# The first tile's decay factors: picked as logarithms for two chunks at once, masked by a product, and the opening of the kernel put into another order

## The chip, the cores and the metric

The kernel runs on one core of a Trainium2 chip. The metric is the device time of one execution in microseconds (us); several executions are timed and their median is taken. Engines are called as in the profile: PE (TensorE, with PEld for its weight loads), DVE (VectorE), ACT (ScalarE), POOL (GpSimd), SP (SyncE, which here only issues DMAs).

## What is computed

A state-space attention over 4 batches and 8 heads, in chunks of the 768 positions, then two feed-forward blocks on the 3072 tokens.

```python
cum = np.cumsum(la, axis=-1)                       # la = log(clip(a))
L = np.exp(cum[:, :, :, None] - cum[:, :, None, :]) * causal
M = np.einsum('bhin,bhjn->bhij', Cc, Bc) * L
y_intra = np.einsum('bhij,bhjd->bhid', M, xc)
y_inter = np.einsum('bhin,bhnd->bhid', Cc, state) * np.exp(cum)[..., None]
state = decay_full * state + sum_j(B_j x_j decay_from_j)
# x: y as [3072, 256]
h = relu(x @ w_in) ** 2;  x = h @ w_out                # d_ff 2048
h = (x @ w1) * (x @ w2) @ w3;  out = h @ w_out2        # d_ff 1024
```

## The kernel before, in words

Tokens go in 6 tiles of 512, the attention in chunks of 96 positions. Tile 0 needs chunks 0 to 5, which make up units 0, 1, 2 of two chunks each. `startup()` computes them in an order that is written out by hand (everything in it is chained engine by engine by `in_order`). After it `step()` runs phase A of tile 0: for each of 16 slices m of the hidden width `h_mm` (PE, L808, 6 products of 512 columns), relu and square (ACT, L822 and L830), a split of the square into a high part (ACT, L838) and a low part (DVE, L139), and `x2_mm` (PE, L855, 6 products) some slices later. Matrices are handled as a high and a low fp32r part, three products for one.

**Weights.** They come as 64-bit words in pieces of 512 KB (`conv_load`, tile names `ua`, then `uo`, `u`). A piece is made into two fp32r parts: `conv_words` (ACT, two instructions, L195 and L197, into `cvs` or `cv`), `conv_bits` (DVE, L206 and L209), `conv_parts` (high part by ACT or POOL, L229 and L227, low part by DVE, L139, into `wa`). Startup converts pieces 0 to 2 and takes the words of piece 3; step m converts piece 3 + m and takes the words of piece 4 + m. Piece j is needed by slice j.

**Tile 0 in startup.** `decays_e_first` (L380) makes the logarithms of the decay rows with 27 small fp32 products out of `lp` (the logs) and `m_rel`/`m_oth` (0/1 masks), and ACT's exp writes them to `e_first`; `decays_cols` (L431) makes the other factors, `dec`. For each unit `unit_g0` (L620) makes C times B in four PSUM banks, `unit_gm` copies them to SBUF with the causal mask (two by DVE, L631, two by ACT, L635, and POOL masks these), `chunk_pick` (L646) spreads four heads' rows of `e_first` over the partitions by a product with a 0/1 matrix `pick`, and `chunk_m0` (DVE, L671) multiplies the picked rows with the masked C times B. `chunk_pre` (POOL, L554) scales x and B of a chunk; `chunk_ds` (L703) makes the chunk's state, `chunk_hand` (ACT, L712, four copies) writes it under the next chunk's x, `chunk_y_mm` (L743) makes y and `chunk_out` splits it into `xt`, the input of phase A.

**Tile 1's chunks** 6 to 10 go another way beside phase A: `unit_split` splits B and C of a unit into high and low (`hl`, ACT L142 and DVE L139), SP stores `hl` to DRAM (`hl_d`), and `unit_bc` reads it back in 12 small DMAs (`bt` x6, `cb` x6).

**What sets the order of the loads.** All DMAs are issued by SP, in the program's order (`dma()` keeps it), and a DMA whose source is not ready holds all behind it. They use eight semaphores in turn, so that a DMA is issued only when the one eight places ahead has landed. In the program's order the store of unit 3's `hl` comes right before weight piece 3, then two small loads of `raw`, then the 12 reads of that store, chunk 6's x, weight piece 4, the store of unit 4, and so on.

Of the kernel before, what the change touches and what calls it, by code (L numbers as in the profile page):

```python
# [46 lines left out]
GPB = 4  # L47
TMPB = 6
# [8 lines left out]
def kernel(  # L57
# [93 lines left out]
    cmask = act1.tile([P, P], F32, tag="cmask", name="cmask")[:, :CH]  # L151
# [130 lines left out]
    lp = new_tmp()[:, :192].rearrange("p (k c) -> p k c", k=3)  # L282

    def constants():
        def diagonal(v):
            nc.gpsimd.affine_select(
                out=v, in_=v, pattern=[[0, v.shape[1]], [-1, v.shape[2]]], base=0, channel_multiplier=1,
                compare_op=ALU.not_equal, fill=1.0,
            )

        nc.gpsimd.memset(ident, 0.0)
        diagonal(ident.unsqueeze(1))
        for k, eng in enumerate((nc.vector, nc.gpsimd)):
            eng.tensor_copy(
                pick[k].rearrange("r h (p j) -> r h p j", p=4),
                ident.rearrange("r (p k h) -> r k h p", p=4, k=4)[:, k].unsqueeze(3).to_broadcast([P, H, 4, 32]),
            )
        nc.gpsimd.memset(cmask, 1.0)
        causal(cmask.unsqueeze(1))
# [6 lines left out]
        nc.gpsimd.memset(cb.bitcast(F32), 0.0)  # L306

    def decays_load(k):
# [4 lines left out]
        else:  # L313
            dma(out=m_oth[:, :392], in_=masks[:, 512:904])

    def decays_ln():
# [3 lines left out]
        )  # L320
        warm = const.tile([P, 1], F32, name="warm")
# [50 lines left out]
    e_first = wts.tile([P, 4, CH], F32, tag="w127", name="e_first")  # L372

    def decays_e_first():

        pv = new_mm()[:, :4 * CH].rearrange("r (v i) -> r v i", v=4)

        def put_e(v, p, i, n, *terms):
            for x, (kk, rhs) in enumerate(terms):
                nc.tensor.matmul(  # L380
                    pv[32 * p:32 * p + 32, v, i:i + n], lp[:, kk, :32], rhs, start=(x == 0),
                    stop=(x == len(terms) - 1), skip_group_check=True,
                )
# [148 lines left out]
    def causal(m):  # L532
# [4 lines left out]
            fill=0.0,  # L537
# [49 lines left out]
    def unit_bi(c0, c1):  # L587
        nc.scalar.copy(bi[:, c0:c1, :CH], batch_0[0][:, c0 * CH:c1 * CH].rearrange("p (c i) -> p c i", i=CH))
# [18 lines left out]
    gm = {}  # L607
    GM_PLACE = ("wo0", "wo1", "wo2", "wo3", "wa10", "wa11")
# [16 lines left out]
    def unit_gm(u, i):  # L625

        gm[u, i] = t = wts.tile([P, 2, 4, CH], F32, tag=GM_PLACE[2 * u + i], name="gm")
        for k in range(2):
            ps = g0[u][2 * i + k][:, :4 * CH].rearrange("p (c i) -> p c i", c=4)
            if i == 0:  # L630
                nc.vector.tensor_tensor(  # L631
                    out=t[:, k], in0=ps, in1=cmask.unsqueeze(1).to_broadcast([P, 4, CH]), op=ALU.mult
                )
            else:
                nc.scalar.copy(t[:, k], ps)  # L635
        if i == 1:
            causal(t.rearrange("p q c i -> p (q c) i"))

    picked = {}

    def chunk_pick(g, i):

        k, v = divmod(g, 4)
        picked[g, i] = ps = new_mm()[:, :4 * CH].rearrange("p (h i) -> p h i", h=4)
        for h in range(4):
            nc.tensor.matmul(  # L646
                ps[:, h], pick[k][:, 4 * i + h], e_first[:, v], start=True, stop=True, skip_group_check=True,
            )

    def unit_e0(u):  # L650
        if u < 2:
            t = at.tile([P, 2, H * CH], F32, tag="e", name="e")
            tiles = [t[:, 0], t[:, 1]]
        else:
            tiles = [wts.tile([P, H * CH], F32, tag=f"w12{2 + k}", name="e") for k in range(2)]
        for g, t in zip(UNITS[u], tiles):
            es[g] = t.rearrange("p (h i) -> p h i", h=H)

    def chunk_e(g, i):

        u, j = UNIT[g]
        if g not in es:
            e = at.tile([P, 2, H * CH], F32, tag="e", name="e")
            for k, gg in enumerate(UNITS[u]):
                es[gg] = e[:, k].rearrange("p (h i) -> p h i", h=H)
        chunk_pick(g, i)
        nc.scalar.copy(es[g][:, 4 * i:4 * i + 4], picked.pop((g, i)))

    def chunk_m0(g, i):
        u, j = UNIT[g]  # L670
        nc.vector.tensor_tensor(  # L671
            out=es[g][:, 4 * i:4 * i + 4].rearrange("p (q h) i -> p q h i", q=2),
            in0=picked.pop((g, i)).rearrange("p (q h) i -> p q h i", q=2), in1=gm[u, i][:, :, 2 * j:2 * j + 2, :],
            op=ALU.mult,
        )
# [22 lines left out]
    def chunk_ds(g, s):  # L698
# [3 lines left out]
        for q in range(4):  # L702
            keep(nc.tensor.matmul(  # L703
                s[32 * q:32 * q + 32], pb[:n, q], xb[:n, 64 * q:64 * q + 64],
                start=True, stop=True, skip_group_check=True,
            ))
# [31 lines left out]
    def chunk_y_mm(g, ys):  # L738
        ch = chs[g]
        for hg in range(2):  # L740
            for q in (2, 3, 0, 1):
                h = 2 * q + hg
                keep(nc.tensor.matmul(  # L743
                    ys[32 * q:32 * q + 32, hg], ch["xb"][:, 32 * h:32 * h + 32], es[g][:, h],
# [14 lines left out]
    def chunk_y(g):  # L759

        yp = y_bank[:, g % 2 * 256:g % 2 * 256 + 256]
        ys, s = yp[:, :2 * CH].rearrange("p (h i) -> p h i", h=2), yp[:, 2 * CH:]
# [3 lines left out]
        if g + 1 == FIRST[2]:  # L766
            s2 = y_bank[:, 448:512]
# [237 lines left out]
    def attention_plan_1():  # L1005
# [26 lines left out]
    def startup():  # L1032
        ys = {}

        def y0(g):
            ys[g] = ps_acc.tile([P, 512], F32, tag="acc", name="y")[:, :2 * CH].rearrange("p (h i) -> p h i", h=2)
            chunk_y_mm(g, ys[g])

        s = y_bank
        ds = [s[:, 64 * (g % 4):64 * (g % 4) + 64] for g in range(FIRST[1])]  # L1040
        constants()
# [3 lines left out]
        batch_load(0)  # L1045
        batch_load(1)
        chunk_xb(0)
        conv_load(1)
        chunk_xb(1)
        chunk_xb(2)  # L1050
        for g in range(3, FIRST[1]):
            chunk_xb(g, f"w12{1 + g}")
        unit_load(4)
        conv_load(1)
        for u in range(3):
            unit_e0(u)
        decays_ln()
        nc.vector.tensor_copy(halves, m_oth[:, 384:392].rearrange("p (q h) -> p h q", h=2)[:, :, 0])
        for q in range(1, 4):
            nc.vector.tensor_tensor(  # L1060
                out=halves, in0=halves, in1=m_oth[:, 384 + 2 * q:386 + 2 * q], op=ALU.add
            )
        nc.scalar.copy(bi[:, :, CH:], id2.unsqueeze(1).to_broadcast([P, FIRST[1], 32]))
        decays_e_first()
        unit_bi(0, 2)
        unit_pad(0)
        decays_cols()
        unit_g0(0)
        unit_bi(2, 6)
        unit_pad(1)  # L1070
        conv_load(1)
        unit_load(5)
        chunk_pre(0)
        unit_gm(0, 0)
        unit_gm(0, 1)
        chunk_pre(1)
        unit_pad(2)
        chunk_pick(0, 0)
        chunk_pick(0, 1)
        unit_g0(1)  # L1080
        chunk_ds(0, ds[0])
        chunk_m0(0, 0)
        chunk_pick(1, 0)
        chunk_m0(0, 1)
        chunk_hand(0, ds[0])
        unit_gm(1, 0)
        unit_gm(1, 1)
        chunk_pre(2)
        unit_split(3, "w120")
        unit_rows(bt)  # L1090
        conv_load(1)
        unit_bc(3)
# [211 lines left out]
```

## Time and profile before

| | |
|---|---|
| time, median of 3 | 567.51 us (567.03 to 569.09) |
| span of the profiled execution | 566.8 us |
| first product of phase A | at 30.88 us |
| first cast of tile 0's result `x` (end of its phase A) | at 94.60 us |
| PE busy | 549.4 us, 97% of the span |
| DVE, ACT, POOL busy | 363.3, 291.9, 90.8 us |

The profiled execution lies 0.7 us below the median. Times in the rows count from the span's start. Busy shares are means over stages with different limits, so the first 100 us are read by stretches below. A line "x16" of a fp32 product counts two instructions for each product of the program, a fp32r product is one.

### The profile page before, as it was taken

What the parts mean: (1) busy time and instruction counts of PE and PEld (TensorE: products, weight loads), DVE (VectorE), ACT (ScalarE), POOL (GpSimd) and SP (SyncE); (2) the same over time, 40 slices, a digit from 0 to 9 for tenths busy, and PEclk for the clock granted to TensorE, in tenths of its full rate; (3) what the DMA queues carried; (4) which work ended last, traced back from release to release, by engine and by line L of the source; (5) the groups of instructions that cost most, each with busy time, mean ns of one, the idle gap of its engine ahead of it and who ended that gap; (6) DMA issues with size and microseconds to landing.
All of it is one profiled execution on the core that took longest, in us unless ns stands there. A gap on an engine that the chain in (4) does not pass through costs nothing.

```text
span 566.8 us, 9839 instructions
## 1 busy us (share of the span) xinstructions
PE 549.4 (97%) x3682; PEld 465.0 (82%) x3682; DVE 363.3 (64%) x651; ACT 291.9 (52%) x579; POOL 90.8 (16%) x138
## 2 busy tenths in 40 slices
PE   6999979999999999999999999999999999999997
PEld 5877757789988888888888988888888888888887
DVE  4888999887999564466666465655466474545431
ACT  5899857877976242263433354333444333544332
POOL 5636650000000212004021004020002010000000
PEclk9999999999999999999999999999999999999999
DMA  8697692043354652057251066120072220100001
GB/s 224 194 321 205 209 378 86 8 162 127 126 193 118 147 138 76 1 139 172 64 123 43 1 164 153 43 78 1 21 195 79 57 71 1 38 1 0 1 2 37
DMA packets 48560, 59.51 MB, mean 105 GB/s; under 512 B 22912, under 2 KB 36608, under 8 KB 48512
## 3 DMA queue, kind: packets, MB, share of 16 engines
q1 hardware_dynamic: 48512, 58.88, 35.9%
q8 instruction: 29, 0.48, 0.4%
q14 instruction: 19, 0.16, 0.1%
HBM read 50.20 MB, written 8.65 MB: 104 GB/s over the span
## 4 chain that ended last, share of the span: by engine, by line
PE 77%; DMA 8%; DVE 8%; SPq 3%; ACT 2%; issue 2%; ACTq 0%; DVEq 0%
PE mm L808 39%; PE acc L855 18%; PE acc L908 10%; PE mm L256 4%; SPq L91 3%; DMA raw<-in_raw_dram 2%; PE y L743 2%; DMA u<-in_w_dram 2%; PE g L599 2%; DMA hl_d<-gp 2%; DVE gp L139 1%; DMA e_d<-tmp 1%; PE mm L646 1%; DVE cvs L206 1%; DVE cvs L209 1%
## 5 line engine op out<-in xcount | busy, mean ns | idle before, releaser
L808 PE MATMUL mm<-xt,wa 128*128 128x512 f32 x576 | 147.2, 393 | 4.2 <-DVE wa L139 3.2
L838 ACT CAST gp<-tmp 128x512 fp32r<-128x512 f32 x144 | 89.5, 621 | 115.4 <-DVE tmp L896 62.8
L855 PE MATMUL acc<-gp,wa 128*128 128x512 f32 x576 | 146.4, 392 | 1.7 <-ACT gp L838 1.1
L139 DVE TENSOR_TENSOR gp<-tmp,gp 128x512 fp32r<-128x512 f32 x144 | 102.5, 712 | 63.3 <-ACT gp L838 63.0
L808 PE MATMUL mm<-x,w 128*128 128x512 f32 x576 | 142.6, 393 | 0.0
L808 PEld LDWEIGHTS mm<-xt,wa 128*128 128x128 f32 x576 | 105.2, 188 | 27.4 <-DVE wa L139 5.3
L855 PEld LDWEIGHTS acc<-gp,wa 128*128 128x128 f32 x576 | 106.3, 188 | 24.1 <-ACT gp L838 1.5
L808 PEld LDWEIGHTS mm<-x,w 128*128 128x128 f32 x576 | 104.5, 188 | 20.5 <-ACT tmp L888 0.2
L822 ACT ACTIVATE tmp<-mm 128x512 f32<-128x512 f32 x96 | 57.3, 597 | 54.7 <-PE mm L808 54.4
L908 PEld LDWEIGHTS acc<-w3o,gp 128*128 128x128 f32 x576 | 75.8, 190 | 4.6 <-DVE gp L139 0.3
L908 PE MATMUL acc<-w3o,gp 128*128 128x256 f32 x576 | 78.5, 283 | 0.1
L832 DVE TENSOR_TENSOR tmp<-tmp 128x512 f32<-128x512 f32 x68 | 47.5, 698 | 30.7 <-ACT tmp L822 30.2
L896 DVE TENSOR_TENSOR tmp<-tmp,mm 128x512 f32<-128x512 f32 x48 | 32.9, 685 | 48.6 <-PE mm L808 44.9
L535 POOL TENSOR_SCALAR_AFFINE_SELECT e<-e 96x768 f32<-96x768 f32 x26 | 25.5, 993 | 234.0 <-DMA e<-e_d 187.8
L888 ACT COPY tmp<-mm 128x512 f32<-128x512 f32 x48 | 28.1, 586 | 45.3 <-PE mm L808 44.8
L554 POOL TENSOR_TENSOR xb<-xb,dec 96x256 f32<-96x256 f32 x32 | 23.5, 733 | 101.0 <-DMA xb<-in_xb_dram 44.2
L605 DVE TENSOR_TENSOR e<-g,e 128x384 f32<-128x384 f32 x52 | 27.6, 550 | 6.0 <-PE g L599 4.7
L256 PE MATMUL mm<-wo,w 128*128 128x256 f32 x128 | 23.6, 283 | 0.3 <-DVE w L139 0.3
L733 DVE SCALAR_TENSOR_TENSOR xb<-xb,through,y 32x64 f32<-32x64 f32 x72 | 20.4, 283 | 3.1 <-PE y L703 1.4
L256 PEld LDWEIGHTS mm<-wo,w 128*128 128x128 f32 x128 | 20.7, 191 | 1.7 <-DVE w L139 0.8
L599 PEld LDWEIGHTS g<-cb,bt 96*128 96x128 f32 x96 | 16.1, 190 | 4.1 <-issue 0.9
L256 PE MATMUL mm<-wo2l,w 128*128 128x256 f32 x64 | 18.1, 283 | 0.0
(99 smaller groups left out, 461.1 us busy)
## 6 DMA issues: line engine op xcount, KB each, us to landing
u<-in_w_dram SPq DMA_DIRECT2D x24, 512.0 KB, 4.3
ua<-in_w_dram SPq DMA_DIRECT2D x16, 512.0 KB, 7.0
e<-e_d SPq DMA_DIRECT2D x40, 192.0 KB, 5.1
xb<-in_xb_dram SPq DMA_DIRECT2D x32, 192.0 KB, 5.0
bt<-hl_d SPq DMA_DIRECT2D x78, 48.0 KB, 2.0
hl_d<-gp SPq DMA_DIRECT2D x9, 384.0 KB, 2.5
cb<-hl_d SPq DMA_DIRECT2D x66, 48.0 KB, 2.0
out_dram<-tmp SPq DMA_DIRECT2D x10, 256.0 KB, 2.6
```

The costliest lines, as they stand in the source:

```text
L139: return nc.vector.tensor_tensor(out=lo, in0=src, in1=hi.bitcast(F32), op=ALU.subtract)
L256: nc.tensor.matmul(acc[:, :DM], v[:, l, e % 4 * P:(e % 4 + 1) * P], wo2[1 + e // 2][r][:, e % 2 * DM:(e % 2 + 1) * DM], start=(n == 0), st ...
L599: nc.tensor.matmul(ps[:, 2 * pp:2 * pp + 2], w, un["c2"][:, pr, :, j * CH:(j + 1) * CH], start=True, stop=True)
L605: nc.vector.tensor_tensor(out=m, in0=ps, in1=m, op=ALU.mult)
L808: i = nc.tensor.matmul(ps, w[m][:, l, col + k * P:col + (k + 1) * P], rhs[k][:, r, :], start=((l, r, k) == (1, 0, 0)), stop=((l, r, k) == ...
L822: nc.scalar.activation(r, ps, AF.Relu)
L832: nc.vector.tensor_tensor(out=g32, in0=r, in1=r, op=ALU.mult)
L838: nc.scalar.copy(g[:, 0, :], d[k])
L855: i = nc.tensor.matmul(acc["x2", t][e], wa[m][:, l, 256 + e * P:256 + (e + 1) * P], g[:, r, :], start=(m == 0 and n == 0), stop=(m == MF - ...
L888: nc.scalar.copy(s, ps)
L896: nc.vector.tensor_tensor(out=p32, in0=prods[t, m], in1=ps, op=ALU.mult)
L908: i = nc.tensor.matmul(acc["o"][sub // per][:, sub % per, :], g[:, l, sub * P:(sub + 1) * P], w3o[m // 2][:, r, m % 2, :], start=(m == 0 a ...
```

## The change

- **Logs instead of factors.** `e_first` holds the picked rows' logarithms as a high and a low fp32r part (`[P, 2, 4, CH]`, ACT writes the high one, DVE the low one); exp comes after picking. For each quarter of a unit (`unit_e1`: two heads, both chunks) one fp32r product `ident` x `nmask` puts -30000 above the diagonal, and four fp32r products of 192 columns add the picked high and low parts for both chunks in the same PSUM bank; ACT's exp writes the result to SBUF. `unit_m0` (DVE) multiplies it with C times B straight from PSUM. `unit_gm`, its copies, its masks on POOL and `cmask` are gone. Chunks 6 and 7 use `unit_e1` without the mask.
- **The rows of `e_first`** are 16 products of 96 columns instead of 27 of mixed widths; for this `decays_ln` makes four small copies of `lp` (`lp2`) on ACT before the exp table is loaded. Four neighbouring products now write four different partition groups.
- **Dummies.** Two fp32 products of 512 columns on zeroes are the first work of PE.
- **Copies.** `chunk_hand` is one copy of 32x256 instead of four of 32x64 (also in phase A); the zeroing of `cb`, the copies into `bi` and the one for unit 0 go to DVE.
- **Loads and order.** The masks' second load is cut in two, B and C of batch 0 are loaded first for 256 positions and then for the rest; the list in `startup()` is written anew.

```diff
-    e_first = wts.tile([P, 4, CH], F32, tag="w127", name="e_first")
+    e_first = wts.tile([P, 2, 4, CH], F32R, tag="w127", name="e_first")
     def decays_e_first():
         pv = new_mm()[:, :4 * CH].rearrange("r (v i) -> r v i", v=4)
...
+        for v in range(4):
+            w = lp[:, v * 2 // 3, :4 * H] if v % 3 == 0 else lp2[:, v - 1]
+            for p in range(4):
...
+                nc.tensor.matmul(pv[32 * p:32 * p + 32, v], w, m, start=True, stop=True, skip_group_check=True)
+        nc.scalar.copy(e_first[:, 0], pv)
+        nc.vector.tensor_tensor(out=e_first[:, 1], in0=pv, in1=e_first[:, 0].bitcast(F32), op=ALU.subtract)
...
+    def unit_e1(u, q, mask=True):
...
+        if mask:
+            nc.tensor.matmul(
+                ps.rearrange("p (n i) -> p n i", n=4), ident, nmask.unsqueeze(1).to_broadcast([P, 4, CH]),
+                start=True, stop=False, skip_group_check=True,
+            )
+        for h in range(2):
+            for l in range(2):
+                nc.tensor.matmul(
+                    ph[:, h], pick[k][:, 2 * q + h], e_first[:, l, v:v + 2], start=(not mask and l == 0), stop=(l == 1),
+                    skip_group_check=True,
+                )
+        nc.scalar.activation(
+            e0[u][q // 2][:, :, 2 * (q % 2):2 * (q % 2) + 2].rearrange("p j h i -> p h j i"),
+            ps.rearrange("p (h j i) -> p h j i", h=2, j=2), AF.Exp
+        )
+    def unit_m0(u, q):
+        e = e0[u][q // 2][:, :, 2 * (q % 2):2 * (q % 2) + 2]
+        nc.vector.tensor_tensor(
+            out=e, in0=g0[u][q][:, :4 * CH].rearrange("p (j h i) -> p j h i", j=2, h=2), in1=e, op=ALU.mult
+        )
...
-        for q in range(4):
-            copy(chs[g + 1]["xb"][CH:, 64 * q:64 * q + 64], s[32 * q:32 * q + 32])
+        copy(chs[g + 1]["xb"][CH:, :256], s[CH:])
```

The new list of `startup()` is best seen in the built order. **ACT, from unit 1's `cp` on, before**: `hl` (L142) is the high part of unit 3, `gm` and `xb` are the copies named above, `ua_143` is weight piece 0.

```order
L581 ACTIVATE cp<-raw_139,halves 128x192 x2
L712 COPY xb<-y 32x64 x4
L635 COPY gm<-g 128x384 x2
L142 CAST hl<-raw_137 128x192
L142 CAST hl<-raw_139 128x192
L508 CAST bt<-id_94 64x8x32
L712 COPY xb<-y 32x64 x4
L635 COPY gm<-g 128x384 x2
L195 ACTIVATE cvs<-ua_143 128x512
```

ACT now, at the end of unit 2's exps (L656); `wa_462` is the high part of weight piece 0.

```order
L656 ACTIVATE e<-mm 128x2x2x96
L709 COPY xb<-y 32x256
L656 ACTIVATE e<-mm 128x2x2x96
L230 CAST wa_462<-cvs 128x512
L144 CAST hl<-raw_111 128x192
L144 CAST hl<-raw_113 128x192
L509 CAST bt<-id_93 64x8x32
```

Unit 3's high part stood behind the first of five state copies and ahead of all weight conversion; it now stands behind all twelve exps and piece 0. **DVE, around unit 3's low part, before**: L671 is `chunk_m0`.

```order
L671 TENSOR_TENSOR e<-mm,gm 128x384 x2
L631 TENSOR_TENSOR gm<-g,cmask 128x384 x2
L139 TENSOR_TENSOR hl<-raw_137,hl 128x192
L139 TENSOR_TENSOR hl<-raw_139,hl 128x192
L671 TENSOR_TENSOR e<-mm,gm 128x384 x2
```

DVE now; L664 is `unit_m0` of unit 1 and, the second time, of unit 2.

```order
L664 TENSOR_TENSOR e<-g,e 128x2x192 x4
L141 TENSOR_TENSOR xt<-mm,xt 128x2x96 x2
L141 TENSOR_TENSOR wa_462<-cvs,wa_462 128x512
L664 TENSOR_TENSOR e<-g,e 128x2x192 x4
L141 TENSOR_TENSOR hl<-raw_111,hl 128x192
L141 TENSOR_TENSOR hl<-raw_113,hl 128x192
```

The low part stood behind the first 2 of 12 multiplications and now stands behind all 12 and behind the low part of piece 0. **ACT, at the start of phase A, before**: `ua_424` is weight piece 4, L822 is relu, L838 the high part of a square.

```order
L822 ACTIVATE tmp<-mm 128x512
L369 ACTIVATE tmp<-mm 128x384 x2
L830 ACTIVATE tmp<-tmp 128x512
L195 ACTIVATE cvs<-ua_424 128x512
L197 ACTIVATE ua_424<-ua_424 128x512
```

ACT now; `ua_516` is weight piece 4, L818, L826 and L834 are what L822, L830 and L838 were.

```order
L818 ACTIVATE tmp<-mm 128x512
L384 ACTIVATE tmp<-mm 128x384 x2
L826 ACTIVATE tmp<-tmp 128x512
L834 CAST gp<-tmp 128x512
L818 ACTIVATE tmp<-mm 128x512
L196 ACTIVATE cvs<-ua_516 128x512
```

The high part of slice 0 and the relu of slice 1 now stand ahead of piece 4's words.

## Rows read from the trace of the kernel before

**Rows 1.** Page, part 2: PE's busy tenths in 40 slices of 14.2 us.
```profile
PE   6999979999999999999999999999999999999997
```
**Rows 2.** Stretches: from:to, length, busy us PE PEld DVE ACT POOL, PEclk, DMA share, GB/s.
```profile
0.00:10.00 10.00, 4.61 (x124) 4.34 (x124) 3.40 (x8) 4.41 (x8) 5.73 (x18) 1.00 0.79 222
...
30.00:40.00 10.00, 9.66 (x96) 8.38 (x97) 7.54 (x13) 9.14 (x21) 3.12 (x5) 1.00 1.03 326
...
50.00:60.00 10.00, 9.26 (x66) 6.88 (x64) 9.69 (x18) 7.69 (x17) 7.56 (x7) 1.00 0.92 266
...
70.00:80.00 10.00, 8.35 (x58) 6.04 (x57) 10.00 (x15) 6.52 (x12) 7.19 (x9) 1.00 0.99 356
```
**Rows 3.** SP's timeline: start us, us, engine, line, DMA issued, count.
```profile
17.87 0.39 SPq L91 DMA_DIRECT2D hl_d<-hl  x1
...
21.39 2.71 SPq L91 DMA_DIRECT2D bt<-hl_d  x6
24.15 3.81 SPq L91 DMA_DIRECT2D cb<-hl_d  x6
...
28.47 0.43 SPq L91 DMA_DIRECT2D ua<-in_w_dram  x1
...
66.91 0.43 SPq L91 DMA_DIRECT2D ua<-in_w_dram  x1
```
**Rows 4.** Landing, us, of `hl_d` 17.87, `bt` 21.39, `ua` 28.47, `ua` 66.91.
```profile
DMA to landing us min/median/max: 3.5/3.5/3.5
...
DMA to landing us min/median/max: 1.9/1.9/1.9
...
DMA to landing us min/median/max: 4.0/4.0/4.0
...
DMA to landing us min/median/max: 6.6/6.6/6.6
```
**Rows 5.** What SP waited for up to 75 us: total, times, longest.
```profile
SPq L91 <- DVE hl L139: 2.2, 1, 2.2
SPq L91 <- ACT tmp L369: 1.6, 2, 1.0
```
**Rows 6.** ACT's timeline: start us, us, line, op, tiles, form, count, idle before.
```profile
11.29 0.84 ACT L635 COPY gm<-g 128x384 f32<-128x384 f32 x2
...
35.54 0.67 ACT L195 ACTIVATE cvs<-ua 128x512 f32<-128x512 f32 x1
...
73.56 0.70 ACT L195 ACTIVATE cvs<-ua 128x512 f32<-128x512 f32 x1 [0.69 <-DVE gp L139]
...
94.60 1.07 ACT L142 CAST x<-acc 128x512 fp32r<-128x512 f32 x2 [0.38 <-PE acc L855]
```
**Rows 7.** DVE's timeline, same columns.
```profile
9.51 0.55 DVE L583 TENSOR_SCALAR cp<-raw,halves 128x192 f32<-128x192 f32 x2 [1.93 <-DMA raw<-in_raw_dram]
...
16.28 1.56 DVE L139 TENSOR_TENSOR hl<-raw,hl 128x192 fp32r<-128x192 f32 x2 [1.28 <-ACT hl L142]
17.76 1.01 DVE L671 TENSOR_TENSOR e<-mm,gm 128x384 f32<-128x384 f32 x2
```
**Rows 8.** PE's timeline, same columns.
```profile
10.20 0.93 PE L620 MATMUL g<-cp,bi 32*128 32x192 f32 x16 [0.54 <-DVE cp L583]
11.06 2.02 PE L646 MATMUL mm<-e_first,pick 128*128 128x96 f32 x16
...
30.88 1.66 PE L808 MATMUL mm<-xt,wa 128*128 128x512 f32 x6 [0.33 <-ACT xt L142]
...
40.09 0.59 PE L599 MATMUL g<-cb,bt 96*128 96x192 f32 x4
...
41.35 3.02 PE L808 MATMUL mm<-xt,wa 128*128 128x512 f32 x12
```
**Rows 9.** Groups up to 31 us: busy us, mean ns | idle before, releaser.
```profile
L743 PE MATMUL y<-e,xb 128*32 128x96 f32 x96 | 3.2, 252 | 1.5 <-DVE e L671 1.5
L380 PE MATMUL mm<-tmp 128*32 128x96 f32 x16 | 2.9, 351 | 4.7 <-DMA tmp<-in_masks_dram 4.7
```

More of the change, by code (lines that the diff above doesn't have):

```diff
@@ L47 @@
 GPB = 4
+NEVER = -30000.0
+WARM = 2
 TMPB = 6
@@ L289, in diagonal @@
             )
-        nc.gpsimd.memset(ident, 0.0)
-        diagonal(ident.unsqueeze(1))
+        warm = gp.tile([P, 512], F32, tag="gp", name="warm")
+        nc.vector.memset(warm, 0.0)
+        for _ in range(WARM):
+            nc.tensor.matmul(y_bank, warm[:, :P], warm, start=True, stop=True, skip_group_check=True)
+        nc.vector.memset(lp2, 0.0)
+        raw = [new_tmp()[:, :P] for _ in range(2)]
+        nc.gpsimd.memset(raw[0], 0.0)
+        diagonal(raw[0].unsqueeze(1))
+        nc.gpsimd.memset(raw[1][:, :CH], 0.0)
+        causal(raw[1][:, :CH].unsqueeze(1), NEVER)
         for k, eng in enumerate((nc.vector, nc.gpsimd)):
@@ L313, in decays_load @@
         else:
-            dma(out=m_oth[:, :392], in_=masks[:, 512:904])
+            c = (slice(256, 392), slice(0, 256))[k - 2]
+            dma(out=m_oth[:, c], in_=masks[:, 512 + c.start:512 + c.stop])
     def decays_ln():
@@ L320, in decays_ln @@
         )
+        for v, r, k, r_in in ((0, 64, 1, 0), (0, 32, 0, 96), (1, 0, 1, 64), (1, 64, 2, 0)):
+            n = 32 if r == 32 or k == 2 else 64
+            nc.scalar.copy(lp2[r:r + n, v], lp[r_in:r_in + n, k, :4 * H])
         warm = const.tile([P, 1], F32, name="warm")
@@ L623, in unit_g0 @@
                 )
[L625 to L632, printed above, removed]
-                )
[L634 to L657, printed above, removed]
@@ L659, in chunk_e @@
-    def chunk_e(g, i):
-        u, j = UNIT[g]
[L662 to L675, printed above, removed]
+    e0 = {}
@@ L1053, in startup @@
         unit_load(4)
         conv_load(1)
-        for u in range(3):
-            unit_e0(u)
+        constants()
         decays_ln()
[L1058 to L1063, printed above, removed]
@@ L1068, in startup @@
+        unit_e1(0, 1)
+        unit_e1(0, 2)
         unit_g0(0)
+        unit_e1(0, 3)
+        for q in range(4):
+            unit_m0(0, q)
         unit_bi(2, 6)
         unit_pad(1)
[L1071 to L1076, printed above, removed]
-        unit_pad(2)
[L1078 to L1088, printed above, removed]
+        chunk_pre(2)
+        unit_e1(1, 0)
+        state(0)
+        unit_e1(1, 1)
+        conv_words(0)
+        conv_bits(0)
+        value(0)
+        unit_e1(1, 2)
+        unit_g0(1)
+        state(1)
+        unit_e1(1, 3)
+        chunk_pre(3)
+        for q in range(4):
+            unit_m0(1, q)
+        value(1)
+        unit_e1(2, 0)
+        unit_pad(2)
+        state(2)
+        unit_e1(2, 1)
@@ L1089, in startup @@
+        chunk_pre(4)
+        value(2)
+        unit_g0(2)
+        unit_e1(2, 2)
+        state(3)
+        unit_e1(2, 3)
+        conv_parts(0)
+        chunk_pre(5)
+        for q in range(4):
+            unit_m0(2, q)
         unit_split(3, "w120")
```

193 lines of the change are left out of this document (83 added, 110 removed).

## The prediction, made before the changed kernel was run

> **What bounds the kernel now.** I read the whole span first, then the first 100 us by stretches, then the queues of SP, ACT, DVE and PE one after the other. PE is busy at nine tenths or more in nearly every slice from the third on [rows 1], and the change touches nothing after tile 0's phase A except the number of state copies. So the question is when that phase ends: at the first cast of `x`, 94.60 us [rows 6]. What comes later moves with it.
>
> Startup ends at 30.88, when PE gets the first product of phase A [rows 8]. Behind it no one engine decides alone. PE, ACT and the DMA engines are near full from 30 to 40, DVE from 50 to 80 with the DMA engines beside it [rows 2]. The weight pieces come on one queue. Piece 4 is issued at 28.47 and takes 4.0, so it lands at 32.4, three us before ACT takes its words at 35.54. Piece 15 is issued at 66.91 and takes 6.6, so it lands at 73.5, and ACT takes its words at 73.56: no slack is left there [rows 3, 4, 6]. The queue's order matters: unit 3's store goes out at 17.87, waits for DVE's low part, and lands 3.5 later; the 12 reads of it fill SP from 21.39 to 27.96, and only then come chunk 6's x and piece 4 [rows 3, 4, 5, 7].
>
> **The change part by part.**
>
> *The opening.* Before, unit 0's C times B starts at 10.20; its `cp` had waited for `raw` [rows 7, 8]. Now the first loads of B and C carry a third of the bytes, and that wait goes. What is late next is `e_first`: masks at 4.7 [rows 9], 32 instructions of 96 columns. Like L743 they go to four partition groups in turn, and L743 needs 3.2 us for six lots of 16 [rows 9], so about 1.1. Then comes a high part on ACT (half of 0.84 and a little, 0.5 [rows 6]) and a low part on DVE (0.55, like one of L671 [rows 7]): 6.9 to 7.2. The three quarters ahead of unit 0's C times B cost 0.6 each: four fp32r products of 192 columns in 0.44 to 0.59 by L599, and one of 384 in under 0.25 by L808 [rows 8]. So C times B starts at 9.0, a gain of 1.2. The zeroing of `cb` and the copies to `bi` now on DVE lie in its waits for masks and `e_first`; uncovered they would cost about 2.
>
> The dummies: the granted clock reads 1.00 in the first 10 us [rows 2], yet the same fp32 form took 351 ns on average at the start and 252 later [rows 9]. I take it that the dummies remove that, 0.5 us for 32 instructions; the bounds are 0 and 1. The Trainium skill (TensorE: Matmul & The Clock Gate, "What's actually happening") says that the engine's default is the throttled state and that activity releases it. By that rule the dummies help; by the granted-clock column they do nothing, and the sum below ends 0.5 later.
>
> *Picks, masks, multiplications.* PE: 12 picks of 8 instructions at 1.0 (half of 2.02 [rows 8]) become 12 quarters of 0.6, minus 4.8; PE had waits there, so this alone buys nothing. DVE: six copies of `gm` go, 0.47 each by L671's pair [rows 7], minus 2.8. ACT: six copies become 12 exps, 0.4 each [rows 6], plus 2.4, and the five state copies become one instruction each instead of four, a saving I leave out. POOL loses its masks. So startup is now ACT's chain, and it is long because ACT and DVE stand in order:
>
> - Unit 0: the last quarter's products end at 10.6, its exp at 11.1, the last multiplication at 12.0.
> - ACT then has the `bi` copy, two pads, an exp, a state copy and an exp, 0.4 each: 13.4. Then piece 0's words, two at 0.6 [rows 6]: 14.6.
> - DVE stands behind them: two bit steps of 0.7 and y's low part, 16.3, then unit 1's four multiplications, 18.2.
> - PE: y of chunk 2 (after DVE's low part of y of chunk 1), unit 2's C times B (0.9 [rows 8]), two quarters and a state product: 21.1; exp at 21.7.
> - ACT piece 0's high part, 22.2; DVE its low part, 22.9; unit 2's four multiplications, 24.8; unit 3's low part, 0.9 for two with POOL idle (1.56 beside a busy POOL [rows 7]): **25.7**.
> - Chunk 5's y follows; ACT takes piece 1's words and unit 4's high part first. First product of phase A at 27.7 instead of 30.88: **3.2 gained**.
>
> *The loads.* The same rows that end startup earlier send unit 3's store out at 25.7 instead of 17.87, as the order shows on ACT and DVE. It holds SP, and behind it stand piece 3, two loads of `raw`, the 12 reads, chunk 6's x, piece 4 and all later loads. It lands in 2.5 to 3.5 (3.5 with other loads under way [rows 4]), 28.7. The reads took 6.6 [rows 3]; their plain issue is 0.45 each (2.71 for six), so 5.5 to 6.6 now, 34.8. Piece 4 goes out at 35.3 instead of 28.47: **6.8 later**.
>
> Does the queue make this up? After 28 us, up to 75, SP waited for an engine only for the decay rows, 1.6 in all [rows 5], and this in a stretch in which the DMA engines were full [rows 2]. So the loads keep their distances, and piece 15 lands at 73.5 + 6.8 = 80.3.
>
> *Phase A with late pieces.* It starts 3.2 earlier, and its picks for chunks 6 and 7 and its state copies are shorter. But ACT stops at piece 4's words until 39.3 (35.54 before), with two more steps behind it done than before (the third place in the order), worth 1.2. From then on it runs piece by piece and stops again at piece 15's words, 80.3 instead of 73.56. Behind piece 15's words ACT has the low words, a square, a cast, the words of the next piece, a relu, a square and a cast, 8 steps of 0.6 with the words themselves: 85.1. DVE's low part, 0.7: 85.8. Then PE has 36 products of 512 columns in the built order, 0.25 each by L808's 12 in 3.02 [rows 8], 9.0, and two y of 0.5 [rows 9]: 95.8, less 0.3 for the products that need only the high part. First cast of `x` at 95.5 instead of 94.60: **0.9 lost**. In the profile before, the same point came only 21.0 us after piece 15's words, because DVE was behind by then; now DVE has had its waits earlier, and 15.2 are enough.
>
> *Sum.* 566.8 + 0.9 = 567.7 in terms of the profiled execution, and its median lies 0.7 above it: **568.4**. What startup gains, the loads take back.
>
> **The rivals.**
>
> *Faster: the store goes out early enough.* My 25.7 rests on a chain of waits between ACT, DVE and PE. If they overlap better, ACT's plain work from 11.1 to unit 3's high part (9 exps, 8 copies and pads, piece 0's three steps, three y, about 10 us) ends at 21, and the low part can be out at 22: the loads shift by 3.0, they no longer decide, and the 3.2 of startup stay. 567.5 - 3.2 = 564.3. For it: these costs are sums of single rows. Against: unit 2's multiplications stand ahead of the store on DVE and need unit 2's last exp. It decides from a store before about 22.5. Chance 0.25.
>
> *Slower: the late loads crowd.* A read of 48 KB takes 1.9 when little else runs [rows 4], but unit 4's reads and the decay rows stand behind whole weight pieces. If phase A's start and the late pieces no longer alternate, each later piece stops ACT again, and the exps, relus and casts behind it wait too. Each us of further shift of piece 15 is then a us of the end. With the store at 27 and the slow ends of landing and reads (3.5 and 6.6 plus 1.2 for x and an emptied queue) the shift is 10: the end moves 4.1, 571.6. It decides where the shift passes 8.7. For it: piece 15 has no slack before. Against: there are emptier stretches in which the queue may catch up. The Trainium skill (DMA: Bandwidth & Descriptors, "Rules for kernel authors") says to issue a DMA early and to wait for it late. By that rule this order errs, and the slower case gains weight. Chance 0.23.
>
> *The change does not do what it says:* the dummies lift no clock. That is 0.5 on the opening and, through the store, on the end: 568.9, inside the forecast.
>
> **How the numbers follow.** The forecast, 568.4, has 0.52; its own range comes from the shift: a store between 24 and 26.5 and the two ends of landing and reads give 4.0 to 8.4, and the end moves us for us, 565.6 to 570.0. A difference of 0.5%, 2.8 us, is about what can be told from no change, so the forecast counts as "same" whole. The range for 8 in 10 reaches to both rivals' times, since each holds more than 0.2: 564.0 to 571.6. Chances: faster 0.25, same 0.52, slower 0.23.
>
> **What would show it.** Right: first product of phase A near 27.7; the store at 25 to 26 and piece 4's issue near 35; ACT idle 2 us or more ahead of piece 4's words and again at piece 15's, ended by a DMA of `ua`; first cast of `x` within 2 us of 94.6. The gap between them is the loss. Wrong: a store before 22.5 or a piece 4 before 32 (then the time falls); DVE full from 50 on as before, with no waits of ACT for `ua` (then the loads did not decide); or first products later than 30.

## The result: slower by 1.2%

The changed kernel takes 575.1 us (median of 4, 572.86 to 575.9) beside 567.37 for the kernel before on the same chip: a ratio of 1.0122, 95% interval 1.0097 to 1.0147. The ratio is not the quotient of the two medians, which would be 1.0136. The prediction, 568.4 with a range of 564.0 to 571.6, was wrong; what came lies beyond its slower rival. The profiled execution has a span of 574.2, 7.4 more than before, and the first cast of `x` came at 102.17 instead of 94.60 [rows 6], 7.57 later. So, in this execution, all of it arose before the end of tile 0's phase A. Lines have moved by a few: L804 is L808 of before, L851 is L855, L818 is L822, L740 is L743, L702 is L703, L196 is L195, L144 is L142, L141 is L139, L93 is L91. New are L646, the mask's product, L652, the picks of a quarter, L656, its exp, and L664, its multiplication.

Stretches of the changed kernel (columns as in [rows 2]; DMA share and GB/s are the last two, the granted clock stands before them):

```profile
20.00:30.00 10.00, 6.56 (x116) 5.27 (x114) 4.65 (x11) 6.32 (x18) 1.75 (x4) 0.90 0.13 38
40.00:50.00 10.00, 6.45 (x28) 5.24 (x27) 4.28 (x7) 7.23 (x15) 1.20 (x3) 0.83 1.02 330
...
28.00:35.00 7.00, 6.06 (x49) 4.73 (x41) 4.53 (x10) 5.17 (x13) 0.00 (x0) 0.51 0.57 172
45.30:48.70 3.40, 3.40 (x9) 2.59 (x9) 1.89 (x3) 3.21 (x8) 0.61 (x1) 0.53 0.97 306
```

From 20 to 30 the DMA engines are nearly empty (0.13), from 40 to 50 they are full while PE, DVE and ACT all have gaps. And the granted clock, 1.00 before in both of the lower stretches, was at about half (1.2 GHz) from 28 to 35 and again from 45.3 to 48.7. SP's timeline shows why the DMA engines were empty (rows of before: [rows 3]):

```profile
27.80 0.39 SPq L93 DMA_DIRECT2D hl_d<-hl  x1
...
32.42 2.72 SPq L93 DMA_DIRECT2D bt<-hl_d  x6
...
38.57 0.43 SPq L93 DMA_DIRECT2D ua<-in_w_dram  x1
...
77.79 0.43 SPq L93 DMA_DIRECT2D ua<-in_w_dram  x1
```

Unit 3's store went out at 27.80 instead of 17.87, and the queue behind it shifted with it: piece 4 from 28.47 to 38.57, piece 15 from 66.91 to 77.79. ACT's timeline (columns of [rows 6]) shows the price:

```profile
42.58 0.66 ACT L196 ACTIVATE cvs<-ua 128x512 f32<-128x512 f32 x1 [3.23 <-DMA ua<-in_w_dram]
...
80.42 0.67 ACT L196 ACTIVATE cvs<-ua 128x512 f32<-128x512 f32 x1 [4.01 <-DMA ua<-in_w_dram]
...
83.80 0.67 ACT L196 ACTIVATE cvs<-ua 128x512 f32<-128x512 f32 x1
...
102.17 1.07 ACT L144 CAST x<-acc 128x512 fp32r<-128x512 f32 x2 [0.74 <-PE acc L851]
```

These are the words of pieces 4, 14 and 15: two long waits for a weight piece, but the second at piece 14 and not, as foretold, at piece 15, where ACT did not wait. PE's timeline:

```profile
10.29 0.93 PE L620 MATMUL g<-cp,bi 32*128 32x192 f32 x16
11.15 0.45 PE L646 MATMUL mm<-nmask,ident 128*128 128x384 f32 x1
11.44 0.58 PE L652 MATMUL mm<-e_first,pick 128*128 128x192 f32 x4
11.86 0.36 PE L646 MATMUL mm<-nmask,ident 128*128 128x384 f32 x1
...
26.93 1.40 PE L740 MATMUL mm<-e,xb 128*32 128x96 f32 x32 [2.40 <-DVE e L664]
...
30.04 2.93 PE L804 MATMUL mm<-xt,wa 128*128 128x512 f32 x6 [0.94 <-ACT xt L144]
...
44.51 0.69 PE L652 MATMUL mm<-e_first,pick 128*128 128x192 f32 x4 [3.55 <-ACT e L656]
```

Startup gained only 0.84 (30.04 against 30.88), its first six products took 2.93 instead of 1.66 [rows 8], and each fall of the clock came soon after a wait of PE: the first, near 28.1, after 2.40 us of waiting that ended at 26.93, the second, near 45.1, after 3.55 that ended at 44.51. The wait of 0.94 came when the clock had fallen already. Two theories therefore: **L**, the late store delays the weight pieces, and these decide; **C**, the falling clock of TensorE costs the time.

### The profile page after: what moved, and what is told of

The parts are those of the page before. It is cut to its first block, busy times and chain, and to the rows that moved or that the text cites. A ratio compares the mean times of both kernels' runs of the same rounds, so it can differ in the third digit from the quotient of the medians.

```text
span 574.2 us, 9685 instructions
## 1 busy us (share of the span) xinstructions
PE 555.4 (97%) x3612; PEld 466.1 (81%) x3612; DVE 359.4 (63%) x647; ACT 291.2 (51%) x560; POOL 86.5 (15%) x134
## 4 chain that ended last, share of the span: by engine, by line
PE 84%; DMA 8%; DVE 3%; ACT 2%; SPq 2%; issue 1%; DVEq 0%; ACTq 0%
PE mm L804 42%; PE acc L851 19%; PE acc L904 12%; PE mm L257 4%; DMA ua<-in_w_dram 3%; PE y L740 2%; SPq L93 2%; DMA hl_d<-gp 2%; PE g L601 2%; DMA uo<-in_w_dram 1%; PE y L702 1%; PE mm L652 1%; DMA hl_d<-hl 1%; DMA u<-in_w_dram 1%; PE mm L646 1%
## 5 line engine op out<-in xcount | busy, mean ns | idle before, releaser
L804 PE MATMUL mm<-xt,wa 128*128 128x512 f32 x576 | 150.5, 399 | 3.9 <-DVE wa L141 2.3
L834 ACT CAST gp<-tmp 128x512 fp32r<-128x512 f32 x144 | 89.4, 621 | 114.7 <-DVE tmp L892 62.7
L851 PE MATMUL acc<-gp,wa 128*128 128x512 f32 x576 | 146.0, 392 | 0.7 <-DVE gp L141 0.4
L804 PE MATMUL mm<-x,w 128*128 128x512 f32 x576 | 142.6, 393 | 0.0
L141 DVE TENSOR_TENSOR gp<-tmp,gp 128x512 fp32r<-128x512 f32 x144 | 101.5, 705 | 64.2 <-ACT gp L834 63.7
L804 PEld LDWEIGHTS mm<-xt,wa 128*128 128x128 f32 x576 | 106.8, 192 | 28.0 <-DVE wa L141 4.5
L851 PEld LDWEIGHTS acc<-gp,wa 128*128 128x128 f32 x576 | 106.4, 188 | 24.1 <-DVE gp L141 1.8
L804 PEld LDWEIGHTS mm<-x,w 128*128 128x128 f32 x576 | 104.5, 188 | 20.4 <-ACT tmp L884 0.2
L818 ACT ACTIVATE tmp<-mm 128x512 f32<-128x512 f32 x96 | 57.1, 596 | 55.7 <-PE mm L804 55.4
L607 DVE TENSOR_TENSOR e<-g,e 128x384 f32<-128x384 f32 x52 | 27.7, 551 | 7.6 <-PE g L601 4.5
L207 DVE SCALAR_TENSOR_TENSOR cvs<-cvs,ua 128x512 uint32<-128x512 uint32 x16 | 13.1, 820 | 10.3 <-ACT ua L198 10.2
```

The source lines that it names most:

```text
L141: return nc.vector.tensor_tensor(out=lo, in0=src, in1=hi.bitcast(F32), op=ALU.subtract)
L607: nc.vector.tensor_tensor(out=m, in0=ps, in1=m, op=ALU.mult)
L804: i = nc.tensor.matmul(ps, w[m][:, l, col + k * P:col + (k + 1) * P], rhs[k][:, r, :], start=((l, r, k) == (1, 0, 0)), stop=((l, r, k) == ...
L818: nc.scalar.activation(r, ps, AF.Relu)
L834: nc.scalar.copy(g[:, 0, :], d[k])
L851: i = nc.tensor.matmul(acc["x2", t][e], wa[m][:, l, 256 + e * P:256 + (e + 1) * P], g[:, r, :], start=(m == 0 and n == 0), stop=(m == MF - ...
```

## The experiments

Ratios are to the kernel before, timed beside each run on the same chip (its median was 567.37 to 568.71 there), so rows are compared by ratios. The last two columns are of the one execution of each run that was profiled. It can lie off the median: below it in e1, f1 and d1, above it in g1, s1, e2 and the change.

| run | median us | ratio, 95% interval | profiled execution, us | first cast of `x` |
|---|---|---|---|---|
| the change | 575.1 | 1.0122 (1.0097 to 1.0147) | 575.9 | 102.17 |
| e1_store_18 | 568.76 | 1.0010 (0.9986 to 1.0033) | 567.47 | 93.86 |
| e1b_store_15 | 569.14 | 1.0001 (0.9985 to 1.0018) | 569.27 | 94.96 |
| e4_hold_clock | 574.66 | 1.0093 (1.0066 to 1.0120) | 574.62 | 99.82 |
| e5_before_late_store | 577.78 | 1.0138 (1.0103 to 1.0173) | 577.39 | 103.50 |
| e2_weights_first | 568.13 | 0.9991 (0.9982 to 1.0001) | 571.17 | 93.62 |
| f1_parts_behind | 566.77 | 0.9964 (0.9951 to 0.9977) | 566.12 | 91.85 |
| f2_early_work | 568.65 | 1.0009 (0.9991 to 1.0027) | 568.78 | 94.86 |
| g1_no_mask_product | 569.73 | 1.0022 (1.0010 to 1.0034) | 571.52 | 98.54 |
| p1_parts_only | 572.49 | 1.0068 (1.0049 to 1.0088) | 571.69 | 96.78 |
| d1_no_dummies | 567.79 | 0.9974 (0.9958 to 0.9990) | 567.25 | 92.88 |
| s1_four_copies | 570.0 | 1.0018 (0.9997 to 1.0039) | 572.41 | 96.36 |
| c1_both_loads | 566.98 | 0.9964 (0.9948 to 0.9980) | 567.15 | 93.12 |

### The loads or the clock

**e1_store_18** moves five lines of the new list forward (e1b_store_15 puts the same lines ahead of unit 1's first exp):

```diff
         conv_bits(0)
+        unit_split(3, "w120")
+        unit_rows(bt)
+        conv_load(1)
+        unit_load(5)
+        unit_bc(3)
         value(0)
...
-        unit_split(3, "w120")
-        unit_rows(bt)
-        conv_load(1)
-        unit_load(5)
-        unit_bc(3)
```

> The changed kernel with one block moved forward in the list of startup: the split of unit 3, its rows, weight piece 3, two loads of raw and the reads of unit 3 now stand right behind the bit steps of piece 0, so that the store goes out about where it did in the kernel before (17.87 us). Theory L (the late store holds SP, and the late weight pieces cost the 7.6 us): store at 17 to 19, piece 4 issued at 28 to 30 instead of 38.57, no wait of ACT for ua over 1 us before 50 us, first cast of x at 94 to 96, time 566 to 569. Theory C (the granted clock of TensorE, 0.5 from 28.2 to 35.0 and from 45.3 to 48.7 us, costs it): the waits of PE at the end of startup stay, the clock falls again, time 572 or more.

> As e1_store_18, with the block still further forward, behind the pads of unit 1 and ahead of its first exp. Theory L: store at 14 to 16, piece 4 issued at 25 to 27; DVE is full from 50 us on, so little is won over e1_store_18: 565 to 568. If ACT's chain of unit 1 decides in startup, the extra 1.0 us on ACT ahead of it comes back as a later first product of phase A (31 us). Theory C: 572 or more.

Both came back to the time of before. SP's timeline of e1_store_18, and its stretch from 30 to 40:

```profile
17.86 0.39 SPq L93 DMA_DIRECT2D hl_d<-hl  x1
...
27.61 0.43 SPq L93 DMA_DIRECT2D ua<-in_w_dram  x1
```

```profile
30.00:40.00 10.00, 9.00 (x62) 7.21 (x63) 6.95 (x13) 8.03 (x19) 1.84 (x3) 0.73 0.80 244
```

Store and piece 4 went out as before, ACT had no wait for `ua`, and 1.1% of the 1.2% were gone, although the clock fell as in the changed kernel (0.73 over this stretch). That is theory L. Sending the store out 3.2 earlier still (e1b, at 14.63) won nothing more; its first product of phase A came at 31.04, and its time lies 1.1 above the range expected.

**e5_before_late_store** does the reverse to the kernel before: the split of unit 3 and the loads behind it in the queue go behind the second multiplication of chunk 4.

```diff
         chunk_m0(4, 1)
+        unit_split(3, "w120")
+        unit_rows(bt)
+        conv_load(1)
+        unit_bc(3)
         chunk_out(3, ys[3])
+        chunk_xb(6)
         conv_load(1)
...
```

(not shown: the lines taken out, and unit 4's split with the loads up to piece 7, which follow later).

> The kernel before, with only this moved: the split of unit 3, its store and reads, and behind them in the queue chunk 6's x, piece 4, unit 4's store and pieces 5 to 7, all to where the changed kernel has them, behind the second multiplication of chunk 4. Nothing of the new decays is in it. Theory L: store at 25 to 28, piece 4 issued at 35 to 39, a wait of ACT for ua of 2 us or more, first cast of x at 99 to 102, time 572 to 576. Theory C, or any cause in the new instructions themselves: PE has no new waits in startup, the clock stays at 1.00, time 567 to 569.

Its SP and ACT:

```profile
27.93 0.39 SPq L91 DMA_DIRECT2D hl_d<-hl  x1
...
36.75 0.43 SPq L91 DMA_DIRECT2D ua<-in_w_dram  x1
```

```profile
43.08 0.66 ACT L195 ACTIVATE cvs<-ua 128x512 f32<-128x512 f32 x1 [5.08 <-DMA ua<-in_w_dram]
```

Not one instruction of the new decays, and it lost 1.4% (9.4 us by the medians), a little more than expected, with a still longer wait for piece 4. Its clock fell too, to 0.83 from 30 to 50, so it does not by itself separate the two theories; e1 does. The Trainium skill (DMA: Bandwidth & Descriptors, "Rules for kernel authors") says to issue a DMA early and wait for it late; the runs agree, with this 1.4% for a piece 4 that was issued at 36.75 instead of 28.47.

**e4_hold_clock** fills PE's wait with ten products without use (`hold(10)` ahead of `value(3)`, each `ident` x `nmask`).

> The changed kernel with ten more fp32r products of 384 columns without use on PE, ahead of chunk 3's y, where PE waited 2.40 us for DVE; nothing else moves. They should keep the granted clock at 1.00 up to 40 us. Theory L: PE's first products of phase A take 1.6 instead of 2.93, but ACT then only waits longer for piece 4 (5 us instead of 3.2), piece 4 is issued at 38.6 as before, time 574 to 576. Theory C: 571 to 573, 2.2 us of PE's time back (2.93 to 1.66 and 3.02 to 2.13) and more.

The clock stayed at 1.00 up to 40 us, and ACT still stood at piece 4:

```profile
30.00:40.00 10.00, 7.70 (x65) 6.22 (x66) 7.00 (x12) 6.66 (x13) 2.02 (x4) 1.00 0.65 175
```

```profile
41.82 0.66 ACT L196 ACTIVATE cvs<-ua 128x512 f32<-128x512 f32 x1 [2.44 <-DMA ua<-in_w_dram]
```

It gained 0.4 by the medians and 0.3% by the ratios, whose intervals overlap: they allow nothing as well as some 0.6%. The first fall of the clock is worth little while the loads are late. (Not only the clock moved: the reads of unit 3 also began 1.4 sooner, at 31.05, and piece 4 was issued at 37.59 instead of 38.57.) The Trainium skill (TensorE: Matmul & The Clock Gate, "HAM oscillation — how this bites in real kernels") says that waits between bursts of products can throttle PE, so that the next burst begins slowly; the falls after 2.40 and 3.55 us of waiting agree with that, though a wait was not always followed by a fall (last section).

**e2_weights_first** leaves the store late and takes only weight pieces 3 to 7 out from behind it:

```diff
+        conv_load(5)
         unit_split(3, "w120")
         unit_rows(bt)
-        conv_load(1)
         unit_load(5)
         unit_bc(3)
```

(and the three later calls that loaded pieces 4 to 7 go). These loads waited for no engine: SP issued them from 10.06 us on.

> The changed kernel with weight pieces 3 to 7 taken out of their places behind the store of unit 3 and put ahead of it in SP's order (they go out from about 11 us on); unit 3's split, store and reads stay as late as they are. Theory L1 (it is the weight pieces behind the store that cost): ACT has no wait for ua at piece 4, but pieces 8 and 9 still stand behind the reads; half or more of the loss comes back, 567 to 571. Theory L2 (it is the reads of unit 3, which chunks 6 and 7 need, or the later pieces 8 to 15 that cost): 573 or more.

0.9991: all of the loss is back with the store at 27.10, although the clock fell here too (0.81 from 20 to 30, 0.85 from 30 to 40). So what costs is neither the late rows of unit 3 nor their 12 reads, but the weight pieces that stood behind them.

### What startup could have gained

**f1_parts_behind** is e1_store_18 with `conv_parts(0)` moved behind unit 2's multiplications.

> e1_store_18 with the two parts of weight piece 0 moved behind unit 2's four multiplications (ACT's high part and DVE's low part stood ahead of them; DVE waited 3.20 us for ACT there). Theory W (this wait holds chunk 3's y and with it PE for 2.40 us): PE's wait ahead of chunk 3's y falls to under 1 us, its clock stays at 1.00, first product of phase A at 28 to 28.8 instead of 30.3, time 1 to 2 below e1_store_18, 566.5 to 568. Rival D (DVE is full from 50 us on and gives the end its time): the first product comes earlier, the first cast of x doesn't, 568 to 569.

In the changed kernel DVE had stood still for 3.20 at the low part of piece 0, with unit 2's multiplications and unit 3's low part behind it:

```profile
24.69 0.69 DVE L141 TENSOR_TENSOR wa<-cvs,wa 128x512 fp32r<-128x512 f32 x1 [3.20 <-ACT wa L230]
25.30 1.94 DVE L664 TENSOR_TENSOR e<-g,e 128x384 f32<-128x384 f32 x4
27.16 0.61 DVE L141 TENSOR_TENSOR hl<-raw,hl 128x192 fp32r<-128x192 f32 x2
```

PE of f1_parts_behind, and its stretch from 30 to 40:

```profile
25.40 1.11 PE L740 MATMUL mm<-e,xb 128*32 128x96 f32 x30 [0.27 <-DVE e L664]
...
28.08 1.20 PE L804 MATMUL mm<-xt,wa 128*128 128x512 f32 x4 [1.14 <-ACT xt L144]
```

```profile
30.00:40.00 10.00, 7.33 (x67) 5.83 (x66) 7.42 (x11) 9.59 (x21) 3.04 (x5) 1.00 0.99 308
```

The wait of 2.40 became 0.27, the first product came at 28.08, the clock read 1.00 throughout, and the kernel is faster than the one before (0.9964) and than e1_store_18 (1.0010; the intervals are apart). Rival D fell: the first cast of `x` moved by 2.0, as the first product did (2.2). How much of it is the clock and how much the wait is not shown. The spread of e1's ten executions hints at the clock: the two with a mean clock of 0.993 or 0.994 took 567.47 and 567.79, near f1's 566.12 to 567.02, the other eight, at 0.987 to 0.991, took 568.47 to 573.04.

**f2_early_work** put still more into the gaps (unit 4's split behind chunk 2's y, the words of pieces 1 and 2 earlier).

> f1_parts_behind with more work put into the empty places of DVE and ACT at the end of startup: unit 4's split behind chunk 2's y, the words and bits of pieces 1 and 2 each one place earlier, and chunk 6's x, pieces 4 to 7 and the small loads right behind unit 3's reads. If DVE's total work gives the end of phase A its time (rival D), only what fills its empty 6 us of 20 to 30 us helps: first cast of x at 91 to 93, 564.5 to 566.5. If PE bounds startup and DVE's order was not the point: 567 to 569.

It gave the gain back (1.0009). Its first product came at 28.82, its clock read 0.87 from 30 to 40 and 0.66 from 60 to 70, and the end was later, so "only early work helps" fell too. The clock is not all of it: the one execution with a mean clock of 1.000 took 567.76, where f1 took 566.12 to 566.82 at 1.000.

**g1_no_mask_product** passes `False` for the mask in all twelve `unit_e1` of startup.

> e1_store_18 without the twelve products of ident and nmask (the causal mask of the first six chunks is left out). It prices a term that the prediction put at under 0.25 us each. If PE bounds startup from 8 to 24 us, C times B of unit 0 starts 0.8 earlier and chunk 3's y some 3 earlier, 24 to 25; if DVE and ACT bound it, less than 1.5 of it arrives there. The first cast of x then moves by 1 to 3 if startup gives the end its time, and not at all if DVE does: 565 to 569.

With less work for PE the kernel got no faster than e1_store_18 (1.0022 and 1.0010, overlapping), and its median, 569.73, lies above the range expected. In the profiled execution C times B came 0.5 earlier (8.88 against 9.37), but then PE waited 0.67 (for ACT) at 15.91 and 1.27 (for DVE) at 17.71, and its clock read 0.50 from 20 to 30 and 0.56 from 30 to 40; the first product came at 32.84:

```profile
20.00:30.00 10.00, 8.34 (x82) 6.45 (x85) 3.18 (x7) 3.26 (x9) 1.80 (x4) 0.50 0.67 189
```

This execution, 571.52 at a mean clock of 0.982, is 1.5 us above all nine others (568.87 to 569.99 at 0.990 to 0.994), so its fall of the clock is not that of the typical run. What holds is that PE's products were not all that bound startup: with fewer of them, PE waited for ACT and DVE.

**p1_parts_only** is f1's move alone, in the changed kernel with its late store.

> The changed kernel with only the two parts of weight piece 0 moved behind unit 2's four multiplications; the store of unit 3 stays behind them. This makes the store about as early as the prediction had it (25.7) and takes the wait of 2.40 us from PE. Theory L with the prediction's slope (piece 4 decides us for us once the loads shift by more than 5.9): store at 25.2 to 26, piece 4 issued at 35 to 36, first product of phase A at 28 to 28.5, first cast of x at 95.5 to 98, time 568.5 to 571. If the fall of the clock to 0.5 was most of the loss: clock 1.00 up to 40 us and time 566 to 568. If neither, 573 or more.

```profile
25.54 0.39 SPq L93 DMA_DIRECT2D hl_d<-hl  x1
...
35.31 0.43 SPq L93 DMA_DIRECT2D ua<-in_w_dram  x1
```

```profile
40.10 0.66 ACT L196 ACTIVATE cvs<-ua 128x512 f32<-128x512 f32 x1 [1.38 <-DMA ua<-in_w_dram]
```

Its store stands where the prediction had that of the changed kernel, and so it tests what followed in the sum (below). 0.5% of the loss goes with the wait of DVE, which had also held the store back by 2.3; 0.7% stays with the store at 25.54, and the time is 1.5 above the range expected. p1 and f1 differ only in the place of unit 3's split, its store (25.54 and 18.20) and what follows it in the queue: 1.0068 and 0.9964.

**d1_no_dummies** (`WARM = 0`), **s1_four_copies** (the state's four products into four partition groups and four copies) and **c1_both_loads** (e2's loads) all start from f1_parts_behind.

> f1_parts_behind (566.77) without the two dummy products at the start of PE. Theory of the prediction (they lift the clock for the first products of e_first): those 32 instructions take 350 ns each instead of 249 to 333, startup and the end come 0.5 to 1 later, 567.2 to 568. Rival: the moment at which the full clock is granted is not set by them, and the products of e_first start when lp2 is there, at 5.0: 566.3 to 567.2.

> f1_parts_behind with the state as before: four products into four partition groups and four copies of 32x64 on ACT, in startup and in phase A. Theory P (PE is full from 8 to 24 us, and a state's products cost 0.61 there instead of 0.29): PE gains 0.3 for each of five states, ACT loses 0.5 for each; chunk 3's y comes 0 to 1 earlier, time 566 to 567. Theory K (ACT's chain decides): chunk 3's y comes 0.5 to 1.5 later, 567 to 568.5.

> f1_parts_behind with weight pieces 3 to 7 ahead of unit 3's store in SP's order, as in e2_weights_first (they go out from about 11 us on). Theory D (the loads no longer decide, ACT and DVE are full from 30 and 40 us on): within 1 us of f1_parts_behind, 566 to 567.8. If loads still decide: piece 15 lands 2 or more earlier and the time is 564 to 566. If five pieces at once make the early loads late (raw, x of chunks 2 to 5, unit 3's store): 568 or more.

Without dummies the products of `e_first` began at 4.39 instead of 5.24 and took 366 ns each instead of 333; C times B of unit 0 came at 9.66 in one and 9.64 in the other, the first product of phase A at 28.23 and 28.08. The dummies neither helped nor hurt to a degree that can be told (0.9974 and 0.9964). c1 equals f1: with the store early the loads no longer decide. s1 lies above both its ranges. Its states cost PE 0.32 each again, as before, instead of 0.63 in f1 (s1's line, then f1's):

```profile
11.96 0.32 PE L701 MATMUL y<-xb,pb 128*32 128x64 f32 x8
```

```profile
11.92 0.63 PE L702 MATMUL y<-xb,pb 128*32 128x64 f32 x8
```

But PE then waited 1.10 for ACT and 1.43 for DVE, the clock fell in startup (0.50 from 20 to 30) and the first product came at 31.95, so what the copies on ACT cost stays open. Of its ten runs the two with the highest mean clock, 0.997, took 566.82 and 567.67, the other eight, at 0.987 to 0.991, 569.5 to 572.4; so its median goes with the clock.

## Why the prediction was wrong

| step | predicted | the change | p1_parts_only |
|---|---|---|---|
| C times B of unit 0 | 9.0 | 10.29 | 9.88 |
| store of unit 3 | 25.7 | 27.80 | 25.54 |
| piece 4 issued | 35.3 | 38.57 | 35.31 |
| first product of phase A | 27.7 | 30.04 | 27.77 |
| ACT at piece 4's words | 39.3 | 42.58 | 40.10 |
| ACT at piece 15's words | 80.3 | 83.80 | 78.85 |
| first cast of `x` | 95.5 | 102.17 | 96.78 |

- **The mechanism held in part**: what startup gains, the queue behind the late store takes back (e1, e2, e5). The path did not hold. Piece 15 was to stop ACT at the end; in the change piece 14 did, and in p1, with the store where the sum had it, ACT had no wait for `ua` but 0.42 and 1.38 before 41 us, and the time was 3.9 above the kernel before, where the sum had 0.9. Of the prediction's signs of being wrong one came: first products later than 30 (30.04).
- **The store's time failed** by 2.1. The terms: the opening lost 1.3 (`e_first`'s products took 1.50, not 1.1, and began 0.5 later; the 70 small ones of `decays_cols`, 1.79, which the sum left out, stood ahead of the first quarter and ended some 0.4 after `e_first` was ready); a quarter of a unit cost PE 0.62 to 0.80, mostly 0.80, not 0.6; and the sum had piece 0's low part on DVE at 22.2, where it ran at 24.69. Part of the opening is luck: ten executions with the same opening, to which no edit came near, had this C times B at 9.37 to 10.29, and the change's is the latest.
- **"So startup is now ACT's chain" was the step behind it.** From 10 to 20 us, before and now:

```profile
10.00:20.00 10.00, 9.77 (x136) 8.40 (x136) 6.94 (x14) 8.13 (x25) 7.67 (x14) 1.00 0.98 259
```

```profile
10.00:20.00 10.00, 10.00 (x127) 8.34 (x125) 5.72 (x12) 7.62 (x19) 6.45 (x15) 1.00 0.82 222
```

  PE had next to no waits there before ("PE had waits there", said the sum) and none now, up to 24.5, while ACT waited for the quarters on PE six times, 3.9 in all:

```profile
22.30 0.49 ACT L656 ACTIVATE e<-mm 128x384 f32<-128x384 f32 x1 [1.20 <-PE mm L652]
```

  So unit 2's last exp ended at 24.15 instead of 21.7. DVE's wait of 3.20 ahead of piece 0's low part was in the sum, at some 3 us (there unit 1's multiplications ended at 18.2 and the low part began at 22.2); it began and ended later.
- **The shift failed with it**: 10.1 instead of 6.8. 2.1 of the difference is the store's time, 1.6 its landing: the reads began 4.6 after it (27.80 to 32.42), where 3.0 was counted and 2.5 to 3.5 allowed; reads and `xb` then took 6.15, 0.4 less than counted. This is the slower rival's condition, shift 10, as it was written; it had 571.6 and 0.23.
- **The end of phase A was mis-sized**, in forecast and rival alike: from piece 15's words to the first cast of `x` 15.2 was counted, 18.4 came (17.9 in p1). The sum gave PE 36 products behind piece 15; piece 14, too, was late (words at 80.42), and from 83.8 to 102.2 PE did 61:

```profile
L851 PE MATMUL acc<-gp,wa 128*128 128x512 f32 x36 | 9.5, 399 | 0.1
L804 PE MATMUL mm<-xt,wa 128*128 128x512 f32 x25 | 6.9, 406 | 1.0 <-DVE wa L141 1.0
```

  DVE was nearly full beside it, so which of the two set the 18.4 is not shown:

```profile
83.80:102.20 18.40, 17.25 (x121) 12.92 (x120) 16.86 (x33) 12.82 (x28) 4.46 (x6) 1.00 0.82 308
```

  The sum took it that DVE "has had its waits earlier"; but DVE read 9.91, 10.00 and 10.00 from 50 to 80, and in p1 9.6 to 10.0 up to 100. Together with the 3.5 at piece 15 this is the whole 6.7 between 95.5 and 102.17.
- **The clock was missing.** The sum took 1.00 for granted since before shows it throughout. In the change itself its first fall was worth about 0.3%, not clear of noise (e4); without late loads it may be most of the step from e1 to f1 (1.0010 to 0.9964), which stays open.
- **A state's products** were left out as a saving. Four products into one partition group cost 0.61 to 0.63 at a clock of 1.00, where four into four groups had cost 0.29 to 0.32 (s1 shows that it is the groups):

```profile
L702 PE MATMUL y<-xb,pb 128*32 128x64 f32 x48 | 4.2, 236 | 0.0
```

  48 instructions up to 31 us took 4.2 (1.05 of it the last state, at half clock) where before took 1.8, at nearly the same mean of one (before: 223 ns): the mean doesn't show what no longer overlaps.
- **Of the forecast's range** the upper end was the rival's 571.6, worked out with the mis-sized 15.2. With 18.4 the rival comes to 574.8, near the 575.1 measured. (The forecast's own shift of up to 8.4 adds up to 8.6 from its terms, which changes nothing here.)

## What to carry to other kernels

When a list is written anew, follow first what issues DMAs: a store that waits for a compute engine holds every later load of its queue, and weight pieces behind it should go ahead of it (e2 got the whole loss back by that alone). Put work that waits for another engine (piece 0's low part) behind work that others wait for. After that, count all products still owed at the last late load, not only those of the last piece. And before a stretch is called one engine's chain, look which engine has no gap in it.

## What the runs showed of the hardware

- A wait of PE is not always followed by a fall of the clock. After the same 1.84 us of waiting for ACT, the same eight products took 1.98 in p1 and 1.14 in f1; the granted clock read 0.50 (1.2 GHz) from 34.0 to 37.0 in p1 and 1.00 in f1. What makes the difference is not shown:

```profile
33.93 1.98 PE L652 MATMUL mm<-e_first,pick 128*128 128x192 f32 x8 [1.84 <-ACT tmp L818]
```

```profile
34.23 1.14 PE L652 MATMUL mm<-e_first,pick 128*128 128x192 f32 x8 [1.84 <-ACT tmp L818]
```

- Less work for PE need not be faster: s1 halved the cost of its states and g1 took twelve products away, but PE then waited 0.7 to 1.4 us at a time for ACT and DVE, and the granted clock went to 0.50 from 20 to 30 in the profiled executions. s1 is slower than f1, from which it was made (1.0018 against 0.9964), g1 no faster than e1 (1.0022 against 1.0010). s1 also had more copies on ACT, so how much of this is the clock is not shown.
- The clock's column does not tell all at the very start: it reads 1.00 up to 10 us in every run, but the same 32 instructions of `e_first` took 364 ns each in the change and 249 in e1_store_18, with the same two dummies ahead of them (their four instructions took 3.78 and 3.48 us). What made the difference is not shown:

```profile
L399 PE MATMUL mm<-tmp 128*32 128x96 f32 x32 | 1.5, 364 | 0.0
```

```profile
L399 PE MATMUL mm<-tmp 128*32 128x96 f32 x32 | 0.9, 249 | 0.0
```
